# Two tiles made 32 and 56 bytes longer, so that the tiles behind them start elsewhere in SBUF

## The chip, the cores and the metric

One core of one Trainium2 chip. The time is device microseconds from the start to the end of one execution, the median of several runs. The engines are written as the profile writes them: PE (TensorE, matmuls), PEld (its weight loads), DVE (VectorE), ACT (ScalarE), POOL (GpSimd), SP (SyncE, which issues most DMAs).

## The reference, cut to what matters

A real Fourier transform of `x` (8 x 3072 x 256) over the sequence and over the model dimension, real part only, and behind it a feed-forward layer with 2048 hidden units and a Mish between its two products:

```
X = np.fft.fft(x, axis=1)
X = np.fft.fft(X, axis=2)
a = X.real                              # 8 x 3072 x 256
h = a.reshape(8 * 3072, 256) @ w_in     # 256 -> 2048
g = h * np.tanh(np.log1p(np.exp(h)))    # Mish
out = g @ w_out                         # 2048 -> 256
```

## The kernel before, in words

The transform over the model dimension is folded into `w_in` once, at the start: `make_wc` multiplies the cosine and sine tables with `w_in` and leaves the products as pairs of a high and a low part, `wch` and `wcl` (cosine), `wsh` and `wsl` (sine). `w_out` is split in the same way into `woh` and `wol`. These six tiles are the weights of the main loop, of type float32r, 128 partitions wide. They stand in the pool `const`.

The sequence transform is done per batch `b`: VectorE and GpSimd add and subtract rows (`pair`, `sums`, `last_fold`) into the tiles `F0e`, `F0o`, `F1e`, `F1o`, and TensorE multiplies these with slices of the table `dft` (`transform`, line 365, 24 products a batch of 256 or 258 columns, in plain float32, for which the trace shows two matmul instructions each). The results are split into `ph`, `pl`, `qh`, `ql` (128 x 512, float32r), one set for each of a batch's three chunks of 1024 tokens. `first_chunk` and `other_chunks` do that; where `par` is 0 they pass through the tile `base`.

The main loop runs 384 steps: 8 batches x 3 chunks x 16 slices of 128 hidden units. Each step issues, in this order on TensorE:

- `mm1`: six matmuls of 512 columns into `pa` and `pb` (lines 695 to 697; weights `wch`, `wcl`, `wsh`, `wsl`, moving operands `ph`, `pl`, `qh`, `ql`);
- `mm2`, for the step ten earlier: twelve matmuls of 512 columns into four accumulators (line 725; weights slices of `woh` and `wol`, moving operands halves of `gh` and `gl`).

Beside it VectorE makes the hidden values out of `pa` and `pb` (`make_h`, lines 704 to 706), ScalarE applies Mish (line 810) and, eight steps later, makes the high part `gh` (line 714), and GpSimd the low part `gl` (line 715). So there are 18 matmuls a step, 6912 in all, each with a weight load of its own of 128 columns. Near the end one token of each batch is done apart: `single_h` (lines 765 to 767: weights `wch` and `wcl`, 8 moving columns) and `single_out` (lines 783 to 785: weights of 8 columns, moving operands `woh` and `wol`, 256 columns).

The order of the work is written out by hand, and the tiles have fixed places: within a partition they stand one behind the other in the order in which the pools and tiles are declared, each at the next multiple of 32 bytes. The order in SBUF is `hring`, `xring`, `dft`, small tiles, the six weight tiles, small tiles, the fold tiles `e`, `o`, `F0e` to `F1o`, `base`, `full0`, `full1`, `spare`, and then `ql`, `pl`, `ph`, `qh`, `p0b`, `ot`, `gl`, `gh`. `dft` has 2 x (2 x 258 + 512) floats a partition, that is 8224 bytes (128 x 64 + 32), and `base` has 258 floats, 1032 bytes, which take 1056.

Of the kernel before, what the change touches and what calls it, by code (L numbers as in the profile page):

```python
# [10 lines left out]
F32 = mybir.dt.float32  # L11
# [18 lines left out]
NE = 258  # L30
# [182 lines left out]
def fft_moe(ctx, tc, x, col_d, mids_d, w_in, w_out, cs_d, dft_d, ysel_d, out, single_d):  # L213
# [4 lines left out]
    def pool(name, bufs=1, **kw):  # L218
        return ctx.enter_context(tc.tile_pool(name=name, bufs=bufs, **kw))

    cp = pool("const")
    dp = pool("dram", space=DRAM)
    fp = pool("fold")
# [7 lines left out]
    def ps(tag):  # L231
        return psab.tile([128, 512], F32, tag=tag, name=tag)
# [2 lines left out]
    hring = cp.tile([128, RH, 1024], F32, name="hring")  # L235

    xring = cp.tile([128, 4, 6 * D], F32, name="xring")
    dft = cp.tile([128, 2, 2 * NE + 512], F32, name="dft")
    alt = cp.tile([128, 2], F32, name="alt")
    midc = cp.tile([128, 3, NB], F32, name="midc")  # L240
    wch = cp.tile([128, FF], F32R, name="wch")
# [39 lines left out]
    def fold_part(b, c, y, i, par):  # L281
        return folds[b][c, y][:, par if COSINE[y][i] else 1 - par, i]
# [71 lines left out]
    def const(c, par, sine):  # L354
        if par == 0:
            o = NE * sine
            return dft[:, c, o:o + NE]
        o = 2 * NE + 256 * sine
        return dft[:, c, o:o + 256]

    def transform(dst, lhs, par, sine, mid_lhs=None, halves=(0, 1), **kw):

        last = 1 if mid_lhs is None else 2
        for c in halves:
            T.matmul(dst, lhs(c), const(c, par, sine), **{"start": c == 0, "stop": c == last, **kw})  # L365
        if mid_lhs is not None and 1 in halves:

            n = dst.shape[-1]
            T.matmul(dst, mid_lhs, alt[0:1, None, :].to_broadcast([1, n // 2, 2]), **{**kw, "start": False, "stop": True})
# [3 lines left out]
    def new_chunk(ch):  # L373
        q = {}
        for n in ("ph", "pl", "qh", "ql"):
            q[n] = pqp.tile([128, 512], F32R, tag=n, name=n)
        chunks[ch] = q

    def split_to(hi, lo, src, eng):
        A.copy(hi, src)  # L380
        eng.tensor_tensor(lo, src, hi, op=ALU.subtract)  # L381

    def add_mid(dst, src, i, b):

        pairs = (y[:, :NE].rearrange("p (a s) -> p a s", s=2) for y in (dst, src))
        dst, src = pairs
        V.scalar_tensor_tensor(dst, alt[:, None, :].to_broadcast([128, NE // 2, 2]), midc[:, i, b:b + 1], src,
                               op0=ALU.mult, op1=ALU.add)

    def first_chunk(b, par, part=(0, 1, 2)):  # L390

        ch = 3 * b
        st = folds[b]
        n = NE if par == 0 else 256
        sl = slice(256 * par, 256 * par + 256)
        if 0 in part:
            st["ps", par] = ps("pa"), ps("pb")
        pa, pb = st["ps", par]
        halves = [c for c in (0, 1) if c in part]
        transform(pa[:, :n], lambda c: fold_part(b, c, "e", 0, par), par, 0, None, halves)  # L400
        transform(pb[:, :n], lambda c: fold_part(b, c, "o", 0, par), par, 1, None, halves)
        if b == 0 and par == 1 and 1 in part:

            T.matmul(pb[:, :n], mid0, const(0, 1, 1)[0:1], start=False, stop=True, skip_group_check=True)
        if 2 in part:
            if par == 0:
                new_chunk(ch)
            q = chunks[ch]
            if par == 0:
                base = fp.tile([128, NE], F32, tag="base", name="base")  # L410
                add_mid(base, pa, 0, b)
                pa = base
            split_to(q["ph"][:, sl], q["pl"][:, sl], pa[:, :256], V)
            split_to(q["qh"][:, sl], q["ql"][:, sl], pb[:, :256], V)
            if par == 0:
                V.tensor_copy(ends[:, b:b + 1], pa[:, 256:257])

    def other_chunks(b, par, odd):

        ch = 3 * b + 1  # L420
        if par == 0 and not odd:
            new_chunk(ch)
            for o in range(2):
                full2[o] = fp.tile([128, 512], F32, tag=f"full{o}", name=f"full{o}")
        st = folds[b]
        n = NE if par == 0 else 256
        sl = slice(256 * par, 256 * par + 256)
        pa, pb = ps("pa"), ps("pb")
        y, cos, sin = ("o", 2, 1) if odd else ("e", 1, 2)
        transform(pa[:, :n], lambda c: fold_part(b, c, y, cos, par), par, 0)  # L430
        transform(pb[:, :n], lambda c: fold_part(b, c, y, sin, par), par, 1)

        base = fp.tile([128, NE], F32, tag="base", name="base")
        spare = fp.tile([128, 256], F32, tag="spare", name="spare")
        if par == 0:
            add_mid(base, pa, 1 + odd, b)
        else:
            V.tensor_copy(base[:, :n], pa[:, :n])

        def combine(dst, sg, o):  # L440
            scaled, plain = (base, pb) if odd else (pb, base)
            V.scalar_tensor_tensor(dst, scaled[:, o:o + 256], sg, plain[:, o:o + 256], op0=ALU.mult, op1=ALU.add)

        combine(spare, R3 if odd else -R3, 0)
        q = chunks[ch]
        h, l = ("qh", "ql") if odd else ("ph", "pl")
        split_to(q[h][:, sl], q[l][:, sl], spare, G)
        combine(full2[odd][:, sl], -R3 if odd else R3, 1 if par == 0 else 0)
# [225 lines left out]
    def chunk0(par, part):  # L674
        first_chunk(0, par, (part,))
# [115 lines left out]
    for tau in range(NS + LAG_M):  # L791
# [17 lines left out]
        if tau < NS:  # L809
            A.activation(hring[:, tau % RH], hring[:, tau % RH], AF.Mish)  # L810
            for f in early.pop(tau, []):
                f()
            other_at = OTHER_AT if b else OTHER0_AT
            if r in other_at:
                i = other_at.index(r)
                other_chunks(b, i % 2, i // 2)
            if r in LAST_AT:
                last_chunk(b, LAST_AT.index(r))
            if r == FOLD_AT[b > 0] and b + 1 < NB:
                fold_q = fold_ops(b + 1)  # L820
                pace = sum(cost for cost, _ in fold_q) / (FOLD_AT[2] - r)
                spent = goal = 0.0
            if fold_q:
                goal += pace
                while fold_q and spent + fold_q[0][0] / 2 <= goal + 1e-9 or fold_q and r == FOLD_AT[2]:
                    cost, f = fold_q.pop(0)
                    spent += cost
                    f()
            if b + 1 < NB and r in FIRST_AT:
                first_chunk(b + 1, FIRST_AT.index(r))  # L830
            if tau % NF == P0_AT and tau // NF + 1 < 3 * NB:
                load_p0(tau // NF + 1)
            if b == NB - 1 and r == 20:
                single = single_h()
            if b == NB - 1 and r == 22:
                single_out(single)
# [29 lines left out]
```

## Time and profile before

| what | us |
|---|---|
| median of 3 runs | 1838.26 (1837.71 to 1840.17) |
| the profiled execution | 1837.48 |
| its span, first to last instruction | 1835.7 |
| PE busy, of the span | 1773.7 (97%) |
| PEld / DVE / ACT / POOL busy | 1410.2 / 1229.0 / 903.7 / 1236.4 |
| mean granted TensorE clock | 0.982 |

The span leaves 1.8 us of the profiled execution outside. A matmul's busy time overlaps that of its neighbours, since matmuls are pipelined; what a stream of them costs is read from the distance between their starts.

### The profile page before, as it was taken

What the parts mean: (1) busy time and instruction counts of PE and PEld (TensorE: products, weight loads), DVE (VectorE), ACT (ScalarE), POOL (GpSimd) and SP (SyncE); (2) the same over time, 40 slices, a digit from 0 to 9 for tenths busy, and PEclk for the clock granted to TensorE, in tenths of its full rate; (3) what the DMA queues carried; (4) which work ended last, traced back from release to release, by engine and by line L of the source; (5) the groups of instructions that cost most, each with busy time, mean ns of one, the idle gap of its engine ahead of it and who ended that gap; (6) DMA issues with size and microseconds to landing.
All of it is one profiled execution on the core that took longest, in us unless ns stands there. A gap on an engine that the chain in (4) does not pass through costs nothing.

```text
span 1835.7 us, 20673 instructions
## 1 busy us (share of the span) xinstructions
PE 1773.7 (97%) x7540; PEld 1410.2 (77%) x7540; DVE 1229.0 (67%) x1609; ACT 903.7 (49%) x980; POOL 1236.4 (67%) x653
## 2 busy tenths in 40 slices
PE   5688999999999999999999999999999999998999
PEld 3366778888888888888888888888888888887887
DVE  7566785677856876577856777568865778553552
ACT  2455454455545555455545555455544555452453
POOL 4368885687756876587756876578765877553556
PEclk8789999999999999999999999999999999998999
DMA  4120200200002000100002000020002000000000
GB/s 170 35 76 29 80 26 4 98 1 30 29 1 98 29 1 29 60 39 29 29 1 98 28 3 29 1 98 29 12 18 97 1 29 30 1 29 1 30 24 23
DMA packets 25016, 67.65 MB, mean 37 GB/s; under 512 B 3027, under 2 KB 3258, under 8 KB 24786
## 3 DMA queue, kind: packets, MB, share of 16 engines
q1 hardware_dynamic: 24354, 64.86, 9.6%
q8 instruction: 59, 0.97, 0.2%
q10 hardware_dynamic: 560, 1.47, 0.2%
q14 instruction: 43, 0.35, 0.1%
HBM read 41.07 MB, written 25.25 MB: 36 GB/s over the span
## 4 chain that ended last, share of the span: by engine, by line
PE 90%; POOL 4%; DVE 2%; issue 2%; ACT 1%; DMA 1%; SPq 0%; DVEq 0%; POOLq 0%
PE acc L725 56%; PE pa L695 5%; PE pa L696 5%; PE pb L695 5%; PE pa L697 5%; PE pb L697 5%; PE pb L696 5%; PE pa L365 2%; PE pb L365 2%; POOL gl L715 1%; ACT gh L714 1%; PE pw L518 1%; POOL xring L504 1%; POOL xring L505 0%; DVE hring L704 0%
## 5 line engine op out<-in xcount | busy, mean ns | idle before, releaser
L715 POOL TENSOR_TENSOR gl<-hring,gh 128x1024 fp32r<-128x1024 f32 x384 | 925.6, 2411 | 515.8 <-ACT gh L714 477.2
L714 ACT CAST gh<-hring 128x1024 fp32r<-128x1024 f32 x384 | 402.8, 1049 | 464.4 <-PE acc L725 464.1
L725 PE MATMUL acc<-gh,woh 128*128 128x512 f32 x1536 | 609.0, 396 | 4.0 <-ACT gh L714 2.2
L725 PE MATMUL acc<-gh,wol 128*128 128x512 f32 x1536 | 607.4, 395 | 0.0
L810 ACT ACTIVATE hring<-hring 128x1024 f32<-128x1024 f32 x384 | 407.3, 1061 | 338.1 <-DVE hring L706 312.9
L704 DVE SCALAR_TENSOR_TENSOR hring<-p0b,wc,pa 128x512 f32<-128x512 f32 x384 | 285.3, 743 | 425.6 <-POOL gl L715 411.8
L725 PE MATMUL acc<-gl,woh 128*128 128x512 f32 x1536 | 433.7, 396 | 2.2 <-POOL gl L715 2.2
L725 PEld LDWEIGHTS acc<-gh,woh 128*128 128x128 f32 x1536 | 288.6, 188 | 76.6 <-ACT gh L714 3.5
L725 PEld LDWEIGHTS acc<-gl,woh 128*128 128x128 f32 x1536 | 288.7, 188 | 73.3 <-POOL gl L715 3.5
L725 PEld LDWEIGHTS acc<-gh,wol 128*128 128x128 f32 x1536 | 289.0, 188 | 69.4 <-POOL wol L537 0.4
L705 DVE TENSOR_TENSOR hring<-hring,pb 128x512 f32<-128x512 f32 x384 | 264.1, 688 | 41.1 <-PE acc L725 0.9
L706 DVE TENSOR_TENSOR hring<-hring,pb 128x512 f32<-128x512 f32 x384 | 263.7, 687 | 13.3
L695 PE MATMUL pa<-ph,wch 128*128 128x512 f32 x384 | 162.8, 424 | 4.0 <-DVE hring L704 4.0
L695 PE MATMUL pb<-qh,wsh 128*128 128x512 f32 x384 | 153.4, 399 | 3.0 <-DVE hring L706 2.6
L696 PE MATMUL pb<-ql,wsh 128*128 128x512 f32 x384 | 152.5, 397 | 0.3 <-POOL ql L381 0.3
L697 PE MATMUL pa<-ph,wcl 128*128 128x512 f32 x384 | 152.6, 398 | 0.0
L696 PE MATMUL pa<-pl,wch 128*128 128x512 f32 x384 | 152.6, 397 | 0.0
L697 PE MATMUL pb<-qh,wsl 128*128 128x512 f32 x384 | 152.3, 396 | 0.0
L695 PEld LDWEIGHTS pb<-qh,wsh 128*128 128x128 f32 x384 | 72.9, 190 | 23.8 <-DVE hring L706 6.0
L695 PEld LDWEIGHTS pa<-ph,wch 128*128 128x128 f32 x384 | 72.6, 189 | 23.3 <-DVE hring L704 4.9
L696 PEld LDWEIGHTS pb<-ql,wsh 128*128 128x128 f32 x384 | 72.6, 189 | 18.0 <-POOL ql L381 0.6
L697 PEld LDWEIGHTS pa<-ph,wcl 128*128 128x128 f32 x384 | 72.6, 189 | 17.7
(192 smaller groups left out, 1343.3 us busy)
## 6 DMA issues: line engine op xcount, KB each, us to landing
xring<-x_dram SPq DMA_DIRECT2D x32, 768.0 KB
out_dram<-ot SPq DMA_DIRECT2D x96, 256.0 KB
p0b<-p_d SPq DMA_DIRECT2D x23, 256.0 KB
xring<-w_out_dram SPq DMA_DIRECT2D x8, 512.0 KB
hring<-w_in_dram SPq DMA_DIRECT2D x4, 512.0 KB
dft<-table_dft_dram ACTq DMA_DIRECT2D x1, 1028.0 KB
winr<-w_in_dram SPq DMA_DIRECT2D x2, 512.0 KB
xring<-w_in_dram SPq DMA_DIRECT2D x2, 512.0 KB
```

Source lines behind the costliest of these rows:

```text
L365: T.matmul(dst, lhs(c), const(c, par, sine), **{"start": c == 0, "stop": c == last, **kw})
L504: G.tensor_tensor(t, t, vf, op=ALU.add)
L695: T.matmul(dst, wh[:, fs], q[n + "h"], start=True, stop=False)
L696: T.matmul(dst, wh[:, fs], q[n + "l"], start=False, stop=False)
L697: T.matmul(dst, wl[:, fs], q[n + "h"], start=False, stop=True)
L704: V.scalar_tensor_tensor(h[:, 0:512], p0b[ch], wc0[:, f:f + 1], pa, op0=ALU.mult, op1=ALU.add)
L705: V.tensor_tensor(h[:, 512:1024], h[:, 0:512], pb, op=ALU.add)
L706: V.tensor_tensor(h[:, 0:512], h[:, 0:512], pb, op=ALU.subtract)
L714: A.copy(gh, h)
L715: G.tensor_tensor(gl, h, gh, op=ALU.subtract)
L725: T.matmul(acc[i], w[:, f, 128 * d:128 * d + 128], g[:, 512 * t:512 * t + 512], **kw)
L810: A.activation(hring[:, tau % RH], hring[:, tau % RH], AF.Mish)
```

## The change: two paddings

`dft` gets 32 bytes more a partition (four floats more in each of its two rows) and `base` 56 bytes more; both are then cut to the sizes that they had, so that everything that uses them stays as it is. No instruction is added, removed or moved on any engine. The one instruction with another shape is the DMA that loads `dft`: its side in SBUF is now two rows of 1028 floats a partition with a gap between them, and was one row of 2056.

```
-    dft = cp.tile([128, 2, 2 * NE + 512], F32, name="dft")
+    dft = cp.tile([128, 2, 2 * NE + 516], F32, name="dft")[:, :, :2 * NE + 512]
...
# first_chunk, par == 0
-                base = fp.tile([128, NE], F32, tag="base", name="base")
+                base = fp.tile([128, NE + 14], F32, tag="base", name="base")[:, :NE]
...
# other_chunks
-        base = fp.tile([128, NE], F32, tag="base", name="base")
+        base = fp.tile([128, NE + 14], F32, tag="base", name="base")[:, :NE]
```

Where the tiles start, in bytes past a multiple of 64 and, in brackets, of 256, by the two programs' allocation:

| tiles | read by TensorE as | before | after |
|---|---|---|---|
| `hring`, `xring` | (start only) | 0 (128) | 0 (128) |
| `wch`, `wcl`, `wsh`, `wsl`, `woh`, `wol` | weights of the main loop; moving in `single_out` | 32 (32) | 0 (64) |
| `F0e`, `F0o`, `F1e`, `F1o` | weights of the transforms | 32 (96) | 0 (0) |
| `ph`, `pl`, `qh`, `ql`, `gh`, `gl` | moving operands of the main loop | 0 (0) | 0 (64) |
| `dft`, first row's four slices | moving operands of the transforms | 0, 8, 16, 16 | 0, 8, 16, 16 |
| `dft`, second row's four slices | the same | 16, 24, 32, 32 | 32, 40, 48, 48 |

The slices that a matmul takes out of the weight tiles, and the halves of `gh` and `gl`, lie at multiples of 512 and 2048 bytes within their tiles, so that all of them start as the tile does.

## Rows read from the trace of the kernel before

**Rows 1.** The page: span, busy time, the chain that ended last by engine.

```profile
span 1835.7 us, 20673 instructions
...
PE 1773.7 (97%) x7540; PEld 1410.2 (77%) x7540; DVE 1229.0 (67%) x1609; ACT 903.7 (49%) x980; POOL 1236.4 (67%) x653
...
PE 90%; POOL 4%; DVE 2%; issue 2%; ACT 1%; DMA 1%; SPq 0%; DVEq 0%; POOLq 0%
```

**Rows 2.** Busy time of each engine by stretch; granted clock, DMA share, GB/s last.

```profile
0.00:120.00 120.00, 77.42 (x259) 44.34 (x260) 77.93 (x142) 42.24 (x75) 51.90 (x50) 0.82 0.22 83
120.00:210.00 90.00, 80.14 (x320) 59.47 (x319) 60.43 (x84) 50.32 (x66) 79.88 (x46) 0.98 0.25 88
...
630.00:840.00 210.00, 210.00 (x905) 169.89 (x904) 149.83 (x187) 107.13 (x112) 146.79 (x76) 1.00 0.09 33
```

**Rows 3.** Timeline of PE in one step: start us, us, what.

```profile
601.28 0.40 PE L695 MATMUL pa<-ph,wch 128*128 128x512 f32 x1
...
602.68 0.40 PE L725 MATMUL acc<-gh,woh 128*128 128x512 f32 x1
...
605.48 0.40 PE L695 MATMUL pa<-ph,wch 128*128 128x512 f32 x1
```

**Rows 4.** Short stretches as in rows 2, for their granted clock.

```profile
204.00:207.00 3.00, 3.00 (x9) 2.34 (x8) 2.86 (x5) 1.22 (x2) 2.84 (x2) 0.52 0.76 247
208.00:211.00 3.00, 3.00 (x15) 2.41 (x14) 2.86 (x4) 0.83 (x1) 1.69 (x2) 1.00 0.02 5
...
1692.00:1695.00 3.00, 3.00 (x17) 1.85 (x16) 0.00 (x0) 0.00 (x0) 0.00 (x0) 0.55 0.00 0
1696.00:1699.00 3.00, 3.00 (x26) 2.36 (x25) 0.36 (x1) 0.00 (x0) 0.00 (x0) 1.00 0.03 5
```

**Rows 5.** Timeline of PE, main loop at the lower clock (three matmuls apart).

```profile
206.04 0.63 PE L695 MATMUL pa<-ph,wch 128*128 128x512 f32 x1
...
207.32 0.48 PE L695 MATMUL pb<-qh,wsh 128*128 128x512 f32 x1
```

**Rows 6.** Timeline of PE in `single_out`: first pair four apart, second twelve.

```profile
1694.59 0.41 PE L784 MATMUL pa<-wol,endgh 128*8 128x256 f32 x1
...
1695.44 0.41 PE L785 MATMUL pa<-woh,endgl 128*8 128x256 f32 x1
...
1696.96 0.28 PE L785 MATMUL pa<-woh,endgl 128*8 128x256 f32 x1
...
1698.32 0.28 PE L785 MATMUL pa<-woh,endgl 128*8 128x256 f32 x1
```

**Rows 7.** Timeline of PE in the transforms (x2: two instructions a row).

```profile
1608.77 0.59 PE L365 MATMUL pa<-dft,F0o 128*128 128x256 f32 x2
...
1610.06 0.59 PE L365 MATMUL pb<-dft,F1o 128*128 128x256 f32 x2
```

**Rows 8.** Timeline of PEld in `single_h`.

```profile
1668.15 0.19 PEld L766 LDWEIGHTS pa<-endl,wch 128*128 128x128 f32 x1
1668.26 0.19 PEld L767 LDWEIGHTS pa<-endh,wcl 128*128 128x128 f32 x1
1668.37 0.29 PEld L765 LDWEIGHTS pa<-endh,wch 128*128 128x128 f32 x1
```

**Rows 9.** Timeline of PEld at the start: weights out of `hring`.

```profile
20.57 1.75 PEld L525 LDWEIGHTS pw<-ones,hring 128*128 128x128 f32 x15 [0.24 <-issue]
```

**Rows 10.** Busy time of line 725 alone from 208 us to the end.

```profile
208.00:1836.00 1628.00, 1086.20 (x4404) 827.52 (x4404) 0.99 0.08 31
```

**Rows 11.** Groups of DVE: one writes at 32 past 64, the other at 0.

```profile
L706 DVE TENSOR_TENSOR hring<-hring,pb 128x512 f32<-128x512 f32 x384 | 263.7, 687 | 13.3
...
L530 DVE TENSOR_TENSOR wcl<-pw,wch 128x512 fp32r<-128x512 f32 x4 | 2.7, 684 | 4.3 <-ACT wch L519 4.3
```

**Rows 12.** What SP's queue waited for: us in total, times, longest.

```profile
SPq L484 <- DMA dft<-table_dft_dram: 4.0, 1, 4.0
```

**Rows 13.** Ten microseconds with folds, as in rows 2.

```profile
680.00:690.00 10.00, 10.00 (x45) 8.04 (x44) 9.58 (x12) 5.27 (x5) 7.74 (x7) 1.00 0.01 2
```

## The prediction, on record before the changed kernel ran

> **What bounds the kernel now.** I read the page first: PE is busy 97% of the span, and 90% of the chain that ended last is PE [rows 1]. Then the stretches: from 0 to 120 us PE is busy 77.42 us, from 120 to 210 us 80.14 of 90, and from there on all the time, 210.00 of 210.00 us in the stretch shown [rows 2]. So the first 200 us hang on other engines and on loads, and the 1,630 us behind them on PE alone. There nothing that PE waits for can be removed, and only the distance between its matmuls' starts counts. The timeline of one step gives it: the step begins at 601.28 us, the next at 605.48, and 18 matmuls of 512 columns start between, so 4.20 us / 18 = 233.3 ns each [rows 3]. At the granted clock of 1.00, the higher level of 2.4 GHz, that is 560 cycles for 512 columns: **48 cycles more than one column a cycle** would take (213.3 ns). This change can only act on those 48 cycles.
>
> Three other places say what kind of excess that is. At the granted clock of about 0.5 (the lower level, 1.2 GHz) [rows 4] the same matmuls start 1.28 us / 3 = 426.7 ns apart [rows 5], exactly 512 cycles: the excess is gone. So it isn't work in the array but something in real time, which hides when columns are taken half as fast; the supply of operands fits. In `single_out`, where 256 columns are moved and the weights have only 8, the starts are 0.85 / 4 = 212.5 ns apart at the lower clock, 256 cycles within the rounding, and 1.36 / 12 = 113.3 ns at the higher, 272 cycles [rows 4, 6]: an excess of 16. In the transforms, plain float32, each instruction moves its 256 columns in 1.29 / 6 = 215 ns [rows 7], half as fast a column, and the excess is about 3 cycles of 512. So only the fast type, one column of four bytes a cycle, shows it.
>
> **Is it the addresses?** Here the rows don't decide. For: `single_out` moves `woh` and `wol`, which start 32 bytes past a multiple of 64. 256 columns are 1024 bytes, 16 blocks of 64 bytes if they start on one and 17 if they start in the middle; 17 x 16 cycles are the 272 seen. And 560 is 35 x 16: 32 blocks of moving data and three more. Against: in the main loop the moving operands start on multiples of 64 already (of 256 even), and still have the larger excess. All that the change gives them is another multiple, 64 past 256. What it mends are the weights, and where weight loads are the bound, the start in the middle costs nothing: those of `wch` and `wcl`, 32 past 64, follow each other at 0.11 us [rows 8], and those out of `hring`, on a multiple of 64, 15 in 1.75 us of which the last takes 0.19, (1.75 - 0.19) / 14 = 0.111 us [rows 9]. So the misplaced weights could only slow the main loop by what they take from the moving operands' supply, and the rows also fit an excess that has nothing to do with places: a share that each weight load takes by its width (48 cycles beside a load of 128 columns, 16 beside one of 8).
>
> [...]
>
> **The change part by part.** Instructions: none added, none removed, none moved; each engine's list is the same, so nothing is queued behind anything new and no wait is added.
>
> Weights of the main loop, from 32 past 64 to 0: between nothing and the whole excess. From 208 us to the end there are 4404 matmuls of line 725 [rows 10], twelve a step, so 367 steps, and with six of `mm1` a step, less the ten steps by which `mm2` lags, 4404 x 18 / 12 - 60 = 6546; the granted clock of that stretch is 0.99 on the mean [rows 10], most of what it lacks falls on the single tokens [rows 4], and at the lower clock there is no excess, so I count 6,500. Before 208 us other engines set the pace, and a faster PE is worth nothing. The upper end: the transforms' 215 ns is the smallest distance that this trace shows for 512 cycles of columns, so 233.3 - 215.3 = 18 ns x 6,500 = 117 us. The lower end is no change. I take **nothing, 0 us**, by the row that is nearest to these loads themselves, the pace of 0.11 us with misplaced weights as with placed ones [rows 8, 9]; the upper end stays in the range.
>
> Moving operands of the main loop, from 0 past 256 to 64 past 256: no row has them anywhere else. 0 us taken; the bounds are the 16 cycles that `single_out` shows as its whole excess [rows 6], 6.7 ns x 6,500 = 43 us more, and nothing gained.
>
> Moving operands of `single_out`, weights of the transforms, slices of `dft`: 48 matmuls x 6.7 ns = 0.3 us at most for the first, half of them on the lower clock; the transforms run within 3 cycles of 512 with their weights at 32 past 64 and with slices at 16 and 32 past [rows 7], so 0. (The title's "all" isn't quite what happens: the slices of `dft` still start at 8, 16, 32, 40 and 48 past 64.)
>
> The other engines' reads and writes at new places: VectorE's subtraction into `wcl` at 32 past 64 takes 684 ns, the one into `hring` at 0 687 [rows 11], so places don't show; 0 us. The load of `dft`, now in two pieces a partition: between nothing and what SP's queue waits on it today, 4.0 us [rows 12], once, in the stretch before 200 us. Behind that wait stands the load of two blocks of `w_in` and the store of `mid_d`; I take 0 and keep the 4 us for the range.
>
> Sum: the profiled 1837.48 + 0, which the runs of before put at a median of 1838.26; I forecast 1838.
>
> **The rivals.** (1) The whole excess comes from the weights' place: 560 cycles become about 517, the step 3.88 us, 1838 - 117 = 1721. For it: the excess is gone at half the clock, and 560 and 272 are whole multiples of 16 cycles. Against: the weight loads alone show no cost, and the moving operands are in place already. A part may be given back in the folds, where VectorE is busy 9.58 of 10 us [rows 13]; a step shorter by 8% asks for more than it has there, RH = 9 ring places smooth that out, so 1721 to 1735. (2) One unit of 16 cycles of the three goes, because a weight slice of 512 bytes touches 8 blocks and no longer 9 and the extra one costs as the extra one in `single_out` does: 6.7 x 6,500 = 43 us, 1795. (3) The excess is shared out over the blocks that the weights touch, and one of nine goes: 48 / 9 = 5.3 cycles, 2.2 ns x 6,500 = 14 us, 1824. (4) Slower: what counts is a larger unit than 64 bytes, or the weights' place relative to the moving operands', which today differ by 32 and then by 0. Each matmul's moving operand then begins in the middle of such a unit, or meets the weights' reads more often, and pays the 16 cycles that the only misplaced moving operand of this trace pays: 43 us more, 1881. It decides as soon as that excess exceeds half a nanosecond a matmul (3.7 us / 6,500). Against it: nothing but that no row has this placing.
>
> **How the numbers follow.** A measurement of this kernel tells about 0.2%, 3.7 us, from no change. No change: 0.42. (1) 0.24, (2) 0.10, (3) 0.12, together 0.46 faster, each less likely than the forecast. (4) 0.12 slower. The pace of the weight loads counts for the forecast, the whole multiples of 16 cycles for the rivals. The likeliest case's own range is 1836 to 1842 (the spread of the runs, and 4 us for the load). The range for all, 1715 to 1842, leaves out rival (4) alone, and takes in rival (1) with a distance a little under 215.
>
> **What would show it.** In the profile after, one step of the timeline: 4.20 us for 18 matmuls is the forecast, 3.88 rival (1), 4.08 rival (2), 4.16 rival (3), 4.32 rival (4). In `single_out` 113.3 ns unchanged says that the place of moving operands is nothing, 107 to 109 that it is worth 16 cycles. If the step is shorter and the time isn't, VectorE or GpSimd took over in the folds, and PE's waits there would show on `hring` or `gl`. The forecast is wrong if weight reads take from the moving operands' supply by where they lie, which no row of this kernel isolates.

## The result and the profile after

The changed kernel takes 1798.07 us (1797.13 to 1799.23), the kernel before 1838.41 in the same runs: ratio 0.9779, 95% interval 0.9763 to 0.9796, so 40 us or 2.2% faster. The forecast was no change at 1838; the time lies inside its range (1715 to 1842) and at the size of rival (2), 1795, though, as the experiments show, not for that rival's reason. One execution of e2 (2334.55 us) and one of e3 (5501.69 us) were slow ones and are left out of the times below.

The page after, the same lines as [rows 1]:

```profile
span 1795.9 us, 20673 instructions
...
PE 1734.6 (97%) x7540; PEld 1408.6 (78%) x7540; DVE 1217.4 (68%) x1609; ACT 898.8 (50%) x980; POOL 1239.8 (69%) x653
...
PE 88%; POOL 5%; DVE 3%; issue 2%; ACT 1%; DMA 1%; SPq 0%; DVEq 0%; POOLq 0%
```

The instructions are the same in number, and the kernel is still bound by PE. The timeline of one step after, as [rows 3] (start us, us, what):

```profile
600.43 0.39 PE L695 MATMUL pa<-ph,wch 128*128 128x512 f32 x1
...
604.51 0.39 PE L695 MATMUL pa<-ph,wch 128*128 128x512 f32 x1
```

The step is 4.08 us, and was 4.20: 226.7 ns a matmul, 544 cycles at the granted clock of 1.00 and no longer 560. (The cycle, in the prediction as here, is an estimate from [rows 5]: from 206 to 207.3 us the granted clock is 0.50 and 512 columns take 426.7 ns, 1.2 a ns; with one cycle a column that is the prediction's 1.2 GHz, and twice that, 2.4, at 1.00, where 512 cycles are 213.3 ns. The nearest that a run comes to it at 1.00 is bfloat16 in e8 below, 215.7 ns for 512 columns.) The excess over one column a cycle fell from 48 to 32. Over the steps this is the whole result: from the start of step 27 to the start of the last, step 383, the trace of before has 1799.2 - 206.0 = 1593.2 us, that of after 1760.3 - 207.4 = 1552.9, 40.3 us less. Some 0.7 us of it is the clock: step 27 of before ran in part at the lower level [rows 4, 5] and took 4.86 us, that of after ran at 1.00.

The stretches after, as [rows 2] and [rows 13]; granted clock, DMA share, GB/s last:

```profile
0.00:120.00 120.00, 78.29 (x251) 44.28 (x252) 76.88 (x137) 42.43 (x75) 49.09 (x50) 0.82 0.22 83
120.00:210.00 90.00, 80.20 (x325) 58.89 (x324) 63.63 (x84) 49.15 (x65) 78.12 (x44) 1.00 0.25 88
210.00:420.00 210.00, 210.00 (x927) 173.57 (x926) 157.52 (x201) 108.69 (x115) 161.85 (x88) 1.00 0.10 35
...
670.00:680.00 10.00, 10.00 (x46) 8.29 (x45) 9.69 (x11) 5.10 (x6) 8.53 (x6) 1.00 0.01 2
```

Up to 210 us nothing is gained: step 27 even starts 1.4 us later. Behind that PE is busy without a break as before, in the folds too, where VectorE stands at 9.69 of 10 us: the shorter step was covered. The load of `dft`, now in two pieces a partition, made SP's queue wait longer than the 4.0 us of [rows 12]. What the start loses by that is lost in its spread: step 27 begins at 206.2 us in e1 below, which has the longer wait (5.8 us), and at 212.0 in e2, which has not (4.0).

```profile
SPq L484 <- DMA dft<-table_dft_dram: 5.9, 1, 5.9
```

And `single_out`, the place where moving operands went from 32 past 64 to 0 past 64, got slower. Its timeline after, as the second pair of [rows 6], twelve matmuls apart, and below it that of e1, where `woh`, `wol` and the weights of 8 columns lie as in the changed kernel:

```profile
1660.82 0.28 PE L785 MATMUL pa<-woh,endgl 128*8 128x256 f32 x1
...
1662.22 0.28 PE L785 MATMUL pa<-woh,endgl 128*8 128x256 f32 x1
```

```profile
1697.04 0.28 PE L785 MATMUL pa<-woh,endgl 128*8 128x256 f32 x1
...
1698.40 0.28 PE L785 MATMUL pa<-woh,endgl 128*8 128x256 f32 x1
```

1.40 / 12 = 116.7 ns, and 113.3 before: an excess of 24 cycles, and 16 before. But e1 has 1.36 / 12 = 113.3 ns at the same places, and so have e3 and e7; e2, with these operands where they lie before, has 116.7. So this stretch has two paces, and where its own operands start doesn't settle which it takes; what does, no run shows. A start on a multiple of 64 brought nothing in any of them. (Its weights lie in `F1e` and `F1o`. By the allocation these start 224 past 256 in the kernel before, not 96 as the table of places has it.)

### The profile page after: what moved, and what is told of

Same layout as the page of the kernel before. It is cut to its first block, busy times and chain, and to the rows that moved or that the text cites. A ratio compares the mean times of both kernels' runs of the same rounds, so it can differ in the third digit from the quotient of the medians.

```text
span 1795.9 us, 20673 instructions
## 1 busy us (share of the span) xinstructions
PE 1734.6 (97%) x7540; PEld 1408.6 (78%) x7540; DVE 1217.4 (68%) x1609; ACT 898.8 (50%) x980; POOL 1239.8 (69%) x653
## 4 chain that ended last, share of the span: by engine, by line
PE 88%; POOL 5%; DVE 3%; issue 2%; ACT 1%; DMA 1%; SPq 0%; DVEq 0%; POOLq 0%
PE acc L725 55%; PE pa L695 5%; PE pa L696 5%; PE pa L697 4%; PE pb L695 4%; PE pb L697 4%; PE pb L696 4%; POOL gl L715 2%; PE pa L365 2%; PE pb L365 2%; POOL xring L505 1%; PE pw L518 1%; DVE hring L704 1%; POOL xring L504 1%; ACT gh L714 1%
## 5 line engine op out<-in xcount | busy, mean ns | idle before, releaser
L725 PE MATMUL acc<-gh,woh 128*128 128x512 f32 x1536 | 599.7, 390 | 1.9 <-ACT gh L714 1.0
L725 PE MATMUL acc<-gh,wol 128*128 128x512 f32 x1536 | 598.4, 390 | 0.1
L725 PE MATMUL acc<-gl,woh 128*128 128x512 f32 x1536 | 422.8, 389 | 2.7 <-POOL gl L715 2.7
L706 DVE TENSOR_TENSOR hring<-hring,pb 128x512 f32<-128x512 f32 x384 | 263.6, 687 | 13.3
L697 PEld LDWEIGHTS pb<-qh,wsl 128*128 128x128 f32 x384 | 72.5, 189 | 15.5
```

Of the source, the lines that this page charges most:

```text
L697: T.matmul(dst, wl[:, fs], q[n + "h"], start=False, stop=True)
L706: V.tensor_tensor(h[:, 0:512], h[:, 0:512], pb, op=ALU.subtract)
L725: T.matmul(acc[i], w[:, f, 128 * d:128 * d + 128], g[:, 512 * t:512 * t + 512], **kw)
```

## The experiments

The theory to begin with was the weights' place (W): on a multiple of 64 they take 16 cycles less from the moving operands. Its rivals were the moving operands' own place (M) and the place of the one relative to the other (R).

**One half of the change each (e1, e2), and another distance (e3).** For e1 only `dft` is changed, for e2 only `base`, at both of its places:

```
# e1_dft_only
-    dft = cp.tile([128, 2, 2 * NE + 512], F32, name="dft")
+    dft = cp.tile([128, 2, 2 * NE + 516], F32, name="dft")[:, :, :2 * NE + 512]
# e2_base_only (both places)
-        base = fp.tile([128, NE], F32, tag="base", name="base")
+        base = fp.tile([128, NE + 14], F32, tag="base", name="base")[:, :NE]
# e3_w64_m0: the change, and base longer still
+        base = fp.tile([128, NE + 62], F32, tag="base", name="base")[:, :NE]
```

> Only the first half of the change: dft 32 bytes longer, base as before. The weights then start on multiples of 64 bytes (64 past 256), the moving operands of the main loop 32 past a multiple of 64. Theory W (the weights' place alone takes 16 cycles from the moving operands' supply): step 4.08 us, 1798 us. Rival M (a misplaced moving operand costs 16 cycles as well): step 4.20 us, 1838 us. Rival R (what counts is whether weights and moving operands lie at the same place past 64): they differ by 32 as before, 4.20 us, 1838 us.

> Only the second half: base 56 bytes longer, dft as before. The weights start 32 past a multiple of 64, and now the moving operands do too. Theory W: step 4.20 us, 1838 us. Rival M: 16 cycles more, 4.32 us, 1881 us. Rival R: both at the same place, 4.08 us, 1798 us.

> The change with base 192 bytes longer still: weights 64 past a multiple of 256 as in the changed kernel, moving operands of the main loop on multiples of 256 as before. Theory W: step 4.08 us, 1798 us. If the moving operands' place past 128 or 256 counts, that is if the move from 0 to 64 past 256 has cost something: under 4.08 us.

One step of e1, then of e2, then of e3, each from its own timeline (start us, us, what):

```profile
1000.00 0.40 PE L695 MATMUL pa<-ph,wch 128*128 128x512 f32 x1
1004.20 0.40 PE L695 MATMUL pa<-ph,wch 128*128 128x512 f32 x1
```

```profile
1001.95 0.39 PE L695 MATMUL pa<-ph,wch 128*128 128x512 f32 x1
1006.03 0.39 PE L695 MATMUL pa<-ph,wch 128*128 128x512 f32 x1
```

```profile
1002.71 0.39 PE L695 MATMUL pa<-ph,wch 128*128 128x512 f32 x1
1006.91 0.39 PE L695 MATMUL pa<-ph,wch 128*128 128x512 f32 x1
```

e1, with the weights on multiples of 64, gains nothing: step 4.20 us, 1839.15 us, ratio 1.0003 (0.9994 to 1.0013). e2, with weights and moving operands both 32 past a multiple of 64, has the whole gain: 4.08 us, 1796.44 us (the median of three), ratio 0.9783 (0.9764 to 0.9801). That refutes W, and M too: the moving operands of e2 lie worse by M, and it is faster. R fits both. But e3 has weights at 64 and moving operands at 0 past 256, equal past 64, and is as slow as before (4.20 us; one execution, 1840.38 us). So if the distance counts, it counts past more than 64.

**Streams of matmuls alone (e5, e6).** Kernels without the computation, in which only the places differ and, where it is said, the widths; `p` is the number of weight columns, `n` of moving ones. Each ran once, as did those of e8 and e9. From the kernel of e6:

```
for j in range(rep):
    m = ms[j % len(ms)]
    T.matmul(acc[i % 8][:p, :n], W[w][:, w // 4:w // 4 + p], M[m][:, m // 4:m // 4 + n], start=True, stop=True)
    i += 1
```

> A kernel of matmul streams alone, which leaves out the whole computation (the outputs are zeros): 32 float32r matmuls each with the same weights (tile w followed by its start in bytes past 256) and the same moving operand (tile m followed by its start), for 41 pairs of places, weight columns (128, 96, 64, 32, 8) and moving columns (512 or 256). Theory W: with 128 weight columns and 512 moving ones 226.7 ns between starts where the weights start on a multiple of 64, 233.3 ns where they start 32 past one, whatever the moving operand's place; the excess over 213.3 ns falls with the number of weight columns, to a quarter at 32. Rival M: 6.7 ns more for moving operands at 4, 16 or 32 past 64. Rival R: 226.7 ns where both starts are equal modulo 64 and 233.3 where they differ by 32. If the excess has nothing to do with the weight loads, it is the same for 128 and 8 weight columns.

> Matmul streams alone again, the whole computation left out (the outputs are zeros): 50 streams of 30 matmuls, every tile now on a multiple of 512 bytes, so that the places are known past 512. Theory D (what counts is the distance between the weights' start and the moving operand's start past 256): 226.7 ns between starts wherever that distance is 0 (0/0, 16/16, 32/32, 48/48, 64/64, 96/96, 128/128, 192/192, 256/256, and 256/0), more at every other distance, and the same value for the same distance (64/0, 96/32, 128/64, 192/128). Rival W (the weights' start past 64 alone): 226.7 ns at weights 0, 64, 128, 192, 256, 320, 384, 448 and 233.3 at 16, 32, 48, 96. If the period of the distance is 128 bytes, 128/0 is fast too; if it is 512, 256/0 is not. A distance with less than 226.7 ns would be a better place than the changed kernel's.

In e6 a tile's name gives its start past 512 with letters for digits (a = 0 to j = 9): `wdc` are weights at 32, `mge` a moving operand at 64. The timeline of e6, one row a stream of 30 (the first, 0/0, has 70 and isn't shown); the distance between two rows' starts, over 30, is what one matmul costs:

```profile
20.39 6.97 PE L158 MATMUL acc<-ma,wbg 128*128 128x512 f32 x30
27.20 7.15 PE L158 MATMUL acc<-ma,wdc 128*128 128x512 f32 x30
34.19 7.16 PE L158 MATMUL acc<-ma,wei 128*128 128x512 f32 x30
...
69.16 7.17 PE L158 MATMUL acc<-ma,wbci 128*128 128x512 f32 x30
76.17 7.16 PE L158 MATMUL acc<-ma,wbee 128*128 128x512 f32 x30
...
97.06 7.04 PE L158 MATMUL acc<-ma,wbjc 128*128 128x512 f32 x30
103.94 7.16 PE L158 MATMUL acc<-ma,wcai 128*128 128x512 f32 x30
...
124.73 6.97 PE L158 MATMUL acc<-ma,wcfg 128*128 128x512 f32 x30
131.53 7.15 PE L158 MATMUL acc<-ma,wcii 128*128 128x512 f32 x30
138.53 7.16 PE L158 MATMUL acc<-ma,wdca 128*128 128x512 f32 x30
...
193.69 6.99 PE L158 MATMUL acc<-mbci,wbci 128*128 128x512 f32 x30
200.52 7.00 PE L158 MATMUL acc<-mbjc,wbjc 128*128 128x512 f32 x30
...
221.06 7.16 PE L158 MATMUL acc<-mge,wjg 128*128 128x512 f32 x30
228.05 7.16 PE L158 MATMUL acc<-mbci,wbga 128*128 128x512 f32 x30
235.04 7.16 PE L158 MATMUL acc<-mge,wdc 128*128 128x512 f32 x30
242.04 7.05 PE L158 MATMUL acc<-mbci,wge 128*128 128x512 f32 x30
```

Weights at 16 cost 6.81 / 30 = 227 ns, at 32 6.99 / 30 = 233, at 128 7.01 / 30 = 233.7, at 192 6.88 / 30 = 229, at 256 6.80 / 30 = 226.7, at 288 7.00 / 30 = 233.3, all with the moving operand at 0; weights and moving operand both at 128 6.83 / 30 = 227.7; 96 with 64 and 160 with 128, both 32 apart, 233, and weights at 32 with the moving operand at 64 7.00 / 30 = 233.3. The settled excess of e6's streams with 128 weight columns, from the last ten gaps between starts in each, in cycles over 512, by the distance, that is the weights' start less the moving operand's, past 256 (32/0 is weights at 32, moving operand at 0):

| distance | excess in cycles |
|---|---|
| 0 (both at 0, 32, 64, 96, 128, 192 or 256; also 256/0) | 32 |
| 16 and 240, moving operand at 0 | 32 |
| 32 (32/0, 288/0, 64/32, 96/64, 160/128) | 48 |
| 48, 64, 96, 112, 144, 160, 208, 224 | 47 to 51 |
| 80, 128, 176 | 41 to 48 |
| 192 (192/0, 448/0, 0/64, 64/128, 128/192) | 37 to 38 |

So what decides, at this shape, is the distance between the two starts, with a period of 256 bytes: 256/0 is fast, 128/0 is not, and the same distance gives the same price, within a few cycles, wherever the pair lies, as long as both start on multiples of 32. On other starts it is less clean: 16/16 and 48/48 settle at 40 and 48/16 at 32, in e5 a moving operand at 4 past 256 costs 56, in e9 below weights 4 to 24 bytes behind the moving operand's start cost 40 to 48, and 16/0 settled at 48 in e5 and at 32 in e6, so that not even the same pair has one price there. The pairs on which the argument rests came out alike each time: 0/0 at 32 in four stream kernels, 32/0 and 64/0 at 48 in three. The kernels fit the table: before 32 - 0 = 32, 48 cycles; e1 64 - 32 = 32, 48; e3 64 - 0 = 64, 48; the changed kernel 64 - 64 and e2 32 - 32, both 0, 32 cycles.

e5 also had narrower weights, and there what the prediction weighed as "a share that each weight load takes by its width" falls. Its groups by form:

```profile
L151 PE MATMUL acc<-m,w 128*8 128x512 f32 x64 | 15.0, 394 | 0.0
```

64 matmuls of 512 moving columns with weights of only 8 columns fill 15.0 us, at distances 0 and 32 alike: (15.0 - 0.39) / 63 = 231.9 ns, an excess of 44 cycles. A load of 8 columns leaves more excess than one of 128 at distance 0.

Other shapes don't follow the table. In e5, 32 weight columns settle at 44 cycles at distance 0 and at 64 at distance 32, 64 columns at 42 and 43, 96 columns at 40 and 37; in e6, 64 weight columns at 39 at distance 0 and at 36 at 192. With 256 moving columns beside 128 weight columns, distance 0 is even the dearest of those tried: 32 cycles (0/0 and 32/32, 120.0 ns), against 28 at 32/0 and 25 at 0/32. The table is one for 128 weight columns and 512 moving ones, the shape of the main loop.

**The table put to the test in the kernel (e7, e4).** Both with all of the main loop's weights and moving operands on multiples of 64 (the "all" that the prediction speaks of), at distances 192 and 0:

```
# e7_w64_m128: the change, with
+        base = fp.tile([128, NE + 30], F32, tag="base", name="base")[:, :NE]
# e4_w0_m0: the change, with
+    dft = cp.tile([128, 2, 2 * NE + 540], F32, name="dft")[:, :, :2 * NE + 512]
```

> The changed kernel with base 64 bytes longer still: weights 64 past a multiple of 256, moving operands of the main loop 128 past one, so both on multiples of 64 and 192 bytes apart past 256. Theory D (the distance past 256 decides, by the table of the streams): 37 cycles of excess for that distance, 549 cycles or 228.9 ns a matmul, a step of 4.12 us, some 1812 us, between before and after. Theory W (weights on a multiple of 64 are enough): 4.08 us, 1798 us. What the title of the change says (all on multiples of 64) would give 1798 us as well.

> The change with dft 192 bytes longer still: weights and moving operands of the main loop both on multiples of 256 bytes, distance 0. Theory D: 226.7 ns a matmul, step 4.08 us, 1798 us, the same as the changed kernel. If a start on a multiple of 256 were worth something by itself: less.

A step of e7, then one of e4:

```profile
1002.15 0.39 PE L695 MATMUL pa<-ph,wch 128*128 128x512 f32 x1
1006.27 0.39 PE L695 MATMUL pa<-ph,wch 128*128 128x512 f32 x1
```

```profile
1002.88 0.39 PE L695 MATMUL pa<-ph,wch 128*128 128x512 f32 x1
1006.96 0.39 PE L695 MATMUL pa<-ph,wch 128*128 128x512 f32 x1
```

e7: step 4.12 us, 1812.49 us, ratio 0.9854 (0.9839 to 0.9869), as the table says for distance 192. e4: 4.08 us, 1798.35 us, ratio 0.9775 (0.9758 to 0.9791), no different from the changed kernel. The distance predicts the kernel's time; the multiple of 64 doesn't.

**What kind of matmul shows it (e8).** The same streams with other operands, all with moving operands at 0. The last letter of a weights' name is their place (a = 0, b = 32, c = 64, d = 128); in a name of three letters the second is the kind, `b` for bfloat16 and the others as below (the conditions of the lines are left out):

```
mt = mt[:, 0:1].to_broadcast([128, 512])          # mc, wc: moving one column
mt = mt[:, None, 0:16].to_broadcast([128, 32, 16]) # md, wd
mt = mt[:, None, 0:64].to_broadcast([128, 8, 64])  # me, we
wt = wt[:, 0:1].to_broadcast([128, 128])          # mf, wf: weights of one column
wt, mt = wt[:64], mt[:64]                          # mg, wg
```

> Matmul streams alone, the whole computation left out (the outputs are zeros): 18 streams of 30 matmuls with 128 weight columns and 512 moving ones, at distances 0, 32, 64 and 128 between the starts, in other kinds: bfloat16; the moving operand one column repeated, 16 columns repeated, 64 columns repeated; the weights one column repeated; 64 of 128 rows. If the excess is the supply of four-byte moving columns meeting the weights' reads: bfloat16 near 216 ns at every distance, a repeated moving column near 216 too, and weights of one repeated column without a difference between the distances. If the excess belongs to the float32r matmul itself (its issue, its change of weights): 226.7 ns with a repeated moving column as well. 64 rows: as 128.

Its timeline, one row a stream of 30:

```profile
20.57 7.15 PE L169 MATMUL acc<-ma,wb 128*128 128x512 f32 x30
27.57 7.16 PE L169 MATMUL acc<-ma,wc 128*128 128x512 f32 x30
...
48.02 6.64 PE L169 MATMUL acc<-mba,wbb 128*128 128x512 bf16 x30
54.49 6.64 PE L169 MATMUL acc<-mba,wbc 128*128 128x512 bf16 x30
60.78 6.91 PE L169 MATMUL acc<-mca,wca 128*128 128x512 f32 x30
67.52 6.74 PE L169 MATMUL acc<-mca,wcb 128*128 128x512 f32 x30
74.10 7.42 PE L169 MATMUL acc<-mda,wda 128*128 128x512 f32 x30
81.36 7.47 PE L169 MATMUL acc<-mda,wdb 128*128 128x512 f32 x30
88.66 7.01 PE L169 MATMUL acc<-mea,wea 128*128 128x512 f32 x30
95.51 7.16 PE L169 MATMUL acc<-mea,web 128*128 128x512 f32 x30
102.50 7.11 PE L169 MATMUL acc<-mfa,wfa 128*128 128x512 f32 x30
109.45 7.12 PE L169 MATMUL acc<-mfa,wfb 128*128 128x512 f32 x30
116.40 7.11 PE L169 MATMUL acc<-mfa,wfc 128*128 128x512 f32 x30
123.44 7.11 PE L169 MATMUL acc<-mga,wga 64*128 64x512 f32 x30
130.39 7.16 PE L169 MATMUL acc<-mga,wgb 64*128 64x512 f32 x30
```

bfloat16 takes 6.47 / 30 = 215.7 ns, at distances 0, 32 and 64 alike (settled, an excess of 6 cycles). A float32r matmul whose moving operand is one column repeated settles at 218.7 ns at distance 0 and 219.3 at 32 (13 and 14 cycles; the stream `mca`, `wcb` takes 6.58 / 30 = 219). So most of the excess is not the float32r matmul's own: with one column repeated it falls from 32 and 48 cycles to 13 and 14. That it goes with the supply of new moving columns is the author's reading, which 16 columns repeated, below, don't fit. With the weights one column repeated, the excess is 44 at distances 0, 32 and 64 alike (6.95 / 30 = 231.7 ns): there the distance means nothing. 64 moving columns repeated (256 bytes) and 64 of 128 rows settle as the plain stream does, at 32 and 48 cycles at distances 0 and 32 (over all of their 30 matmuls the two at distance 0 take 6.85 / 30 = 228.3 ns and 6.95 / 30 = 231.7); 16 columns repeated (64 bytes) are worse than anything else in e8, 69 to 72 (7.26 / 30 = 242 ns and 7.30 / 30 = 243).

**Which of the loads it is (e9).** A matmul's weights and those of its successor, loaded while it runs (in the page after PEld is busy 1408.6 us beside PE's 1734.6, in a span of 1795.9), at different distances:

```
w, m = ws[j % len(ws)], ms[j % len(ms)]   # weights and moving operand in turn from two places
```

> Matmul streams alone, the whole computation left out (the outputs are zeros): the weights and the moving operand each taken in turn from two places, so that a matmul's own distance differs from its distance to the weights that are loaded while it runs, those of the next matmul. Weights 0 and 64 in turn with moving operands 0 and 64 in turn: own distance 0, to the next weights 64 either way. The same with moving operands 64 and 0: own distance 64, to the next weights 0. If the next weights' place meets the running matmul's reads: the second pair at 226.7 ns, the first above it. If a matmul's own weights count: the first at 226.7, the second at 230 and more. Beside it weights 4 to 24 bytes before and behind the moving operand. Anything below 226.7 ns would point to a faster placing than the changed kernel's; I expect none.

Each of the two readings forecast 226.7 ns, 32 cycles, for one of the orders; both settled at 45. So neither holds by itself, and which of the loads it is stays open. None of its 50 streams was below 32; for this shape, distance 0 throughout is as good as the best that was found, and the changed kernel has it. No version that beats it came out of the runs; e2 and e4 do the same.

## Why the prediction was wrong, point by point

- **What bounds the kernel** was right: up to 207 us nothing changed, behind it 40.3 us fell out of PE's steps alone. So was the unit: the change could only act on the 48 cycles, and it took 16 of them. That no instruction moves, and that the folds would cover a shorter step, held as well. 6,500 matmuls x 6.7 ns, the product under rivals (2) and (4), gives 43 us; 40.3 were measured (of the steps with transforms in them some fell by 0.07 or 0.08 us and not by 0.12).
- **The step that failed** is adding up the two moves, of the weights and of the moving operands, as terms of their own. Each alone is worth nothing, as the sum had it: weights at 64 with the moving operands left at 0 (e3) take 4.20 us a step, and moving operands at 64 with weights left at 32 (`mge`, `wdc` in e6) 233 ns a matmul. Together they bring the distance from 32 to 0 and take 16 of the 48 cycles, 6.7 ns a matmul. The sum has no term for what the two do together; only rival (4) speaks of it.
- **The row behind the first term**, the pace of the weight loads in `single_h` [rows 8, 9], could not have shown it. Those rows have weight loads that are themselves the bound, 0.11 us apart, with 8 moving columns beside them. They can say whether misplaced weights load more slowly, not what they do to a stream of moving columns that has no slack.
- **The bounds of the second term**, "43 us more, and nothing gained", left out a gain by the moving operands' place. e2 makes no change to the weights, brings the distance to 0 by the moving operands alone (from 0 to 32 past 256), and has it all; e1 moves the weights and the moving operands by 32 each and leaves the distance as it was.
- **Rival (2)** had the time, 1795, and the step, 4.08 us, for a wrong reason: 8 blocks of 64 bytes and no longer 9. e1 has those 8 blocks and gains nothing.
- **Rival (4)** named the right quantity, the weights' place relative to the moving operands', "which today differ by 32 and then by 0", and put the price on the wrong side: 0 is the cheap distance.
- **The reading 272 = 17 x 16** of `single_out` was a coincidence: with its moving operands on a multiple of 64 the excess should have gone, and it was 24 cycles in the changed kernel and 16 in e1. The other reading, a share by the weights' width, fell too (8 columns, 44 cycles). A slip beside it: 215 ns in the transforms are 516 cycles, an excess of 4 and not 3, which changes nothing.
- **Whether the weights' place counts at all** for a stream of moving columns, which no row of before isolated, the streams tell: with nothing but the weights' place changed, from 0 to 32, a float32r stream goes from 226.7 to 233.3 ns (e6); a bfloat16 one stays at 215.7 ns at each of three places (e8).

Shown is that for float32r matmuls of 128 weight columns and 512 moving ones, both on multiples of 32, the distance past 256 decides (32 cycles at 0, 37 to 38 at 192, 48 at 32); that it shows neither in bfloat16 (6 cycles at three distances) nor with weights of one column repeated (44 at three); and that at half the clock a matmul of before takes 426.7 ns, 40 less than twice its 233.3 [rows 3, 5]. Not shown is why: what the two reads share, whether the running matmul's weights or the next one's count, and what makes one and the same placing run at two paces in `single_out` and at 16/0. The 32 cycles that are left, 13.3 ns x 6,500 = 87 us, stayed at every placing tried.

## What to carry to other kernels

Where float32r matmuls follow one another without a wait, compare the distance in time between their starts with that of one column a cycle (here 213.3 ns for 512, by the estimate above; 233.3 before, 226.7 after); if it is longer, look at where weights and moving operands begin. For 128 weight columns and 512 moving ones, bring both to the same place past 256 bytes, on a multiple of 32; for other shapes other places were better here, and streams of matmuls alone tell which. An allocation between the two that grows by 32 bytes shifts one against the other and was worth 2% here (e2, ratio 0.9783), while one ahead of both changed nothing (e1, 1.0003); so the distance is worth an assertion. And two changes that meet in one quantity can't be priced one by one: ask first what they do together. A term is only bounded by a row in which the same thing is the bottleneck: a load's own pace says nothing on what the load does to its neighbour.

## What the runs showed of the hardware that was not expected

- How long a float32r matmul of 128 weight columns and 512 moving ones takes goes by the distance between its two operands' starts, with a period of 256 bytes in e6 (256/0 as 0/0, 288/0 as 32/0). With both on multiples of 32 that is 544 cycles at distance 0, 549 at 192, some 560 at most others.
- Weights of 8 columns (e5), or of one column repeated (e8), don't lower the excess beside 512 moving columns; they put it at 44 cycles at each place tried. Weights of 128 columns at distance 0 are cheaper, 32. Beside 256 moving columns their distance 0 is the dearest of those tried, 32 cycles against 25 and 28.
- A moving operand of one column repeated runs at 218.7 to 219.3 ns, one of 16 columns repeated at 242 to 243 ns, slower than 2048 bytes in a row (226.7 ns). Whether that is the same 64 bytes again and again or the pattern of short rows, no run tells; 64 columns repeated settle at 32 cycles at distance 0, as the plain stream does.
- 64 rows in place of 128 settle at the same 32 and 48 cycles at distances 0 and 32 (e8). In bfloat16 the distance doesn't show (215.7 ns at three distances); plain float32, at the places of the first kernel's transforms, takes 215 ns for 256 columns [rows 7], 4 cycles over 512.
- The same operands at the same places can run at two paces: 113.3 and 116.7 ns in `single_out`.
